# Hash-bucketed attention and a channel mix on one core: the planner's wanted times replaced by one written sequence

## The chip, the core and the metric

The kernel runs on one core of a Trainium2 chip. Five engines matter: PE (TensorE, matmuls), ACT (ScalarE), DVE (VectorE), POOL (GpSimd) and SP (SyncE, which here only issues DMAs). Each engine takes its own instructions in program order; an instruction whose input is not there holds everything behind it on that engine. The metric is the device time of one execution in microseconds (us). Before the change it is 253.47 us, the median of three runs (252.47 to 254.20).

## The reference, cut to what matters

```python
q_bits = (q @ proj > 0); k_bits = (k @ proj > 0)      # q, k, v: (4, 8, 768, 64); proj: (64, 6)
mask   = q_bucket[..., :, None] == k_bucket[..., None, :]   # buckets: the 6 bits as a number
attn   = softmax(where(mask, q @ k.T / 8, -1e9))
x      = (attn @ v), heads side by side: (4, 768, 512)
xk, xr = mu * x + (1 - mu) * x_prev                   # x_prev: the row before
k      = relu(xk @ w_k) ** 2                          # w_k: (512, 1024)
out    = sigmoid(xr @ w_r) * (k @ w_v)                # w_r: (512, 512), w_v: (1024, 512)
```

The 32 heads are worked on in 16 pairs; four pairs (0 to 3, 4 to 7 and so on) make one batch, and one batch can enter the channel mix when its four pairs are through.

## The kernel before, in words

**Work of one pair n.** SP loads q, k (lines 485, 491; names `ldq`n with side q or k) and v (line 496, `ldv`n) in fp32. DVE splits q and k into a high and a low fp16 part (`hi`, line 560; `lo`, line 563), SP transposes them by DMA (`tr`, line 567; one for q, one for k). PE computes the sign bits of the hash (`bits`, line 586), DVE turns them into fp16 values (`bx`, line 589), and four small DMAs put them as extra rows under q and k (`row`, line 599; a and b for the two heads of q, c and d for those of k). Then nine score steps of 1024 columns follow (`sc`, line 702), each with one exponential on ACT (`exp`, line 706). Six groups of matmuls apply v (`oo`, line 732), DVE divides (`rc`, `ob`), the result is transposed (`ot` on PE, line 758, or by a DMA, line 764), and DVE mixes it with the row before (`df`, `xk`, `xr`, lines 789 to 804). For v, POOL adds up the columns (`va`, `vsum`, lines 511 to 523) and PE makes the mean (`mean`, line 536). Pairs 0 and 1 have their q and k transposed by PE instead (lines 620 to 645), and pair 0 gets its bits in place (lines 662 to 670).

**Work of one batch.** 16 groups of four matmuls with w_k (`kp`, line 822), a relu on ACT and a square on DVE for each (lines 826, 829), 6 groups with w_r and a tanh (`r`, lines 841, 844), 12 groups with w_v (`v`, line 851), 6 products on DVE (line 858) and 6 stores (line 861).

**Weights.** w_k comes by four casting DMAs that POOL issues (`wg`, line 446); w_r and w_v come in fp32 by SP (`wl`, line 463) and POOL casts them (line 470).

**What sets the order.** The function writes all 1328 operations with `add(engine, duration, priority, function, reads, writes, ...)`. `Plan.schedule` (lines 159 to 284) then runs through them with a model of time: at each moment each engine takes the ready operation with the lowest wanted time, and the wanted time of operation i is entry i of the list `WANT` (lines 44 to 101). A DMA of more than 0.3 us is held back while the modelled queue has more than `BACKLOG` = 1.5 us of work. The operations are emitted in the order in which the model started them (lines 883 to 886), so the model fixes the order on each engine, and the bank of PSUM that each matmul group writes (`plan.slot`): three pairs of banks for score steps and `bits`, four banks for the rest, of which the channel mix holds at most three.

At most eight DMAs of SP and ACT are in flight, one for each of eight semaphores.

Of the kernel before, what the change touches and what calls it, by code (L numbers as in the profile page):

```python
# [17 lines left out]
LAG = {"PE": 0.30, "ACT": 0.25, "DVE": 0.20, "POOL": 0.20, "SP": 1.8, "GQ": 2.0}  # L18


BACKLOG = 1.5

# [17 lines left out]
def R(kind, n):  # L40
# [3 lines left out]
WANT = [  # L44
    2, 8, 6, 12, 18, 10, 26, 38, 44, 24, 5, 11, 30, 34, 35, 23, 36, 3, 33, 14, 32, 22, 0, 9,
    25, 1, 39, 42, 45, 48, 49, 46, 59, 31, 112, 84, 74, 63, 101, 324, 348, 401, 425, 387, 414, 455, 482, 379,
    403, 446, 470, 4, 41, 13, 37, 102, 21, 7, 117, 47, 50, 52, 51, 65, 66, 53, 19, 58, 40, 54, 17, 68,
    71, 76, 80, 62, 67, 73, 77, 56, 82, 89, 95, 104, 98, 69, 15, 78, 83, 90, 103, 64, 75, 175, 115, 123,
    135, 133, 61, 57, 72, 87, 28, 27, 70, 60, 96, 86, 100, 79, 29, 20, 55, 16, 107, 110, 134, 120, 127, 119,
    106, 131, 43, 91, 99, 105, 81, 88, 118, 109, 122, 132, 113, 130, 125, 129, 97, 141, 144, 148, 121, 157, 159, 154,  # L50
    161, 155, 166, 167, 170, 176, 179, 181, 188, 185, 108, 85, 221, 137, 147, 152, 156, 94, 92, 128, 93, 126, 114, 158,
    169, 194, 174, 187, 173, 172, 145, 150, 163, 164, 171, 178, 162, 153, 168, 142, 146, 143, 160, 139, 151, 138, 140, 190,
    198, 197, 207, 208, 177, 195, 183, 180, 204, 237, 220, 230, 233, 246, 241, 192, 182, 281, 191, 196, 206, 210, 124, 136,
    149, 111, 116, 165, 186, 193, 227, 202, 228, 211, 214, 184, 257, 262, 231, 238, 239, 244, 219, 217, 226, 218, 189, 200,
    205, 216, 201, 199, 267, 268, 271, 274, 275, 234, 236, 242, 252, 253, 279, 288, 297, 305, 300, 311, 203, 229, 298, 240,
    245, 250, 255, 222, 224, 248, 209, 212, 235, 273, 277, 302, 286, 299, 294, 247, 256, 243, 249, 276, 285, 260, 265, 263,
    269, 283, 295, 251, 270, 278, 290, 225, 215, 315, 292, 280, 291, 318, 293, 296, 307, 319, 323, 330, 334, 338, 341, 345,
    349, 350, 357, 362, 374, 383, 393, 392, 420, 424, 428, 434, 437, 380, 386, 398, 417, 427, 435, 433, 441, 448, 495, 504,
    516, 413, 423, 429, 431, 449, 454, 452, 461, 468, 450, 527, 533, 439, 444, 459, 500, 507, 522, 512, 519, 541, 520, 536,
    539, 485, 492, 525, 546, 550, 597, 497, 514, 558, 563, 566, 607, 542, 560, 562, 567, 572, 638, 578, 586, 594, 649, 616,  # L60
    939, 530, 581, 625, 635, 650, 925, 656, 664, 613, 642, 686, 913, 266, 213, 356, 301, 308, 312, 322, 332, 327, 336, 232,
    223, 259, 254, 258, 272, 284, 304, 329, 328, 343, 316, 346, 352, 333, 344, 351, 360, 325, 335, 339, 408, 317, 331, 310,
    289, 313, 321, 303, 309, 402, 407, 405, 418, 421, 363, 367, 369, 372, 375, 340, 467, 494, 506, 502, 543, 503, 517, 337,
    365, 426, 314, 320, 326, 342, 355, 353, 361, 282, 287, 347, 261, 264, 306, 376, 381, 396, 404, 391, 412, 410, 416, 395,
    406, 399, 411, 359, 368, 422, 430, 388, 397, 354, 373, 384, 390, 370, 378, 471, 475, 508, 490, 524, 457, 462, 469, 473,
    478, 371, 599, 620, 626, 637, 641, 629, 639, 477, 364, 532, 377, 382, 385, 438, 440, 443, 463, 358, 366, 415, 389, 409,
    432, 481, 487, 509, 528, 501, 513, 515, 523, 419, 436, 442, 451, 488, 496, 505, 510, 445, 456, 460, 464, 465, 472, 476,
    480, 529, 535, 499, 545, 547, 583, 585, 593, 602, 606, 466, 612, 628, 633, 647, 655, 644, 678, 484, 511, 553, 447, 453,
    458, 474, 483, 479, 486, 498, 491, 518, 394, 400, 489, 551, 559, 574, 569, 584, 565, 549, 554, 538, 540, 557, 576, 651,
    659, 631, 654, 627, 634, 573, 592, 589, 600, 587, 596, 675, 679, 684, 691, 694, 660, 665, 668, 673, 683, 493, 706, 735,  # L70
    739, 743, 749, 746, 753, 808, 817, 825, 819, 828, 834, 788, 801, 810, 779, 787, 809, 827, 839, 848, 849, 857, 865, 833,
    843, 847, 872, 878, 884, 786, 852, 860, 876, 882, 887, 851, 861, 866, 886, 905, 902, 867, 871, 880, 906, 909, 916, 894,
    897, 901, 864, 908, 911, 783, 797, 923, 935, 953, 1003, 769, 784, 919, 940, 945, 952, 962, 968, 955, 966, 973, 995, 988,
    989, 1035, 1039, 1044, 1049, 999, 1005, 974, 992, 1010, 1017, 1048, 1057, 930, 949, 1061, 1063, 537, 580, 652, 548, 552, 556, 577,
    579, 582, 588, 521, 526, 561, 531, 534, 544, 617, 622, 657, 636, 630, 646, 610, 614, 671, 677, 666, 669, 619, 624, 621,
    632, 604, 609, 648, 653, 601, 605, 640, 645, 693, 713, 715, 718, 721, 688, 701, 704, 708, 710, 590, 772, 793, 794, 796,
    803, 800, 806, 570, 591, 643, 568, 571, 575, 663, 670, 667, 676, 555, 564, 623, 603, 611, 661, 705, 712, 737, 729, 750,
    725, 698, 702, 690, 695, 720, 722, 717, 723, 711, 714, 733, 741, 728, 731, 742, 748, 680, 687, 738, 744, 747, 757, 762,
    758, 752, 767, 771, 773, 681, 781, 812, 814, 821, 831, 818, 836, 618, 755, 917, 672, 682, 685, 696, 699, 703, 707, 595,
    598, 674, 608, 615, 692, 724, 730, 740, 760, 766, 778, 813, 820, 782, 792, 770, 776, 822, 829, 775, 790, 763, 768, 754,  # L80
    764, 751, 756, 761, 777, 856, 842, 841, 858, 862, 798, 802, 815, 823, 826, 709, 895, 915, 920, 921, 927, 924, 1054, 732,
    853, 824, 689, 697, 700, 719, 726, 727, 734, 658, 662, 716, 774, 780, 791, 859, 868, 881, 890, 873, 877, 830, 835, 845,
    850, 869, 874, 883, 891, 879, 885, 795, 804, 855, 863, 837, 846, 805, 811, 899, 918, 934, 937, 938, 893, 896, 898, 910,
    912, 736, 959, 976, 979, 981, 985, 1059, 1066, 1076, 1080, 1085, 1047, 1051, 1071, 1072, 1078, 1082, 1062, 1070, 1075, 1124, 1130, 1134,
    1084, 1090, 1101, 1087, 1093, 1098, 1095, 1108, 1115, 1135, 1141, 1144, 1064, 1106, 1111, 1086, 1100, 1104, 1092, 1120, 1123, 1149, 1156, 1158,
    1131, 1137, 1140, 1119, 1125, 1129, 1112, 1127, 1132, 1154, 1162, 1147, 1187, 1194, 1196, 1146, 1152, 1181, 1185, 1186, 1190, 1193, 1200, 1199,
    1206, 1208, 1211, 1217, 1221, 1161, 1170, 1223, 1227, 1224, 1229, 1232, 1238, 1242, 1246, 1220, 1226, 1235, 1234, 1240, 1243, 765, 807, 816,
    936, 941, 944, 961, 967, 970, 977, 759, 745, 844, 889, 892, 903, 943, 948, 965, 969, 956, 991, 947, 951, 926, 933, 900,
    904, 907, 914, 971, 975, 980, 984, 1004, 1009, 922, 928, 997, 1001, 1007, 1008, 1015, 1019, 1026, 1020, 1023, 1027, 1032, 1036, 983,
    1040, 1053, 1056, 1065, 1069, 1073, 1077, 799, 888, 986, 946, 950, 954, 990, 993, 996, 1000, 785, 789, 832, 838, 840, 854, 958,  # L90
    963, 972, 998, 982, 978, 1011, 1018, 987, 994, 1025, 1028, 1030, 1037, 1034, 1046, 1055, 1068, 1081, 1088, 1089, 1103, 1060, 1067, 1058,
    1094, 1107, 1113, 1117, 1122, 1126, 1128, 1133, 1136, 1002, 1139, 1153, 1155, 1157, 1160, 1159, 1163, 957, 960, 964, 1014, 1024, 1021, 1029,
    870, 875, 929, 931, 932, 942, 1097, 1099, 1105, 1116, 1102, 1110, 1045, 1052, 1013, 1022, 1050, 1074, 1118, 1121, 1091, 1096, 1142, 1145,
    1079, 1083, 1109, 1114, 1143, 1148, 1138, 1150, 1151, 1165, 1164, 1166, 1171, 1174, 1177, 1178, 1031, 1182, 1192, 1195, 1201, 1203, 1198, 1230,
    1006, 1012, 1016, 1033, 1038, 1041, 1042, 1184, 1189, 1197, 1202, 1191, 1188, 1180, 1183, 1173, 1175, 1204, 1207, 1168, 1172, 1176, 1179, 1169,
    1167, 1205, 1209, 1212, 1214, 1216, 1210, 1213, 1215, 1218, 1219, 1043, 1222, 1225, 1228, 1231, 1236, 1239, 1233, 1237, 1250, 1244, 1256, 1245,
    1249, 1251, 1255, 1260, 1262, 1248, 1252, 1254, 1261, 1266, 1268, 1258, 1263, 1265, 1264, 1269, 1271, 1253, 1257, 1259, 1278, 1283, 1286, 1273,
# [5 lines left out]

class Op:
    pass


class Plan:

    def __init__(self, pairs, banks, most, moe_most):
        self.ops = []
        self.writer = {}
# [39 lines left out]
    def schedule(self):  # L159
# [31 lines left out]
        t = 0.0  # L191
# [726 lines left out]
```

## Time and profile before

| | |
|---|---|
| time, median of 3 runs | 253.47 us (252.47 to 254.20) |
| the profiled execution: its span, which is the only time recorded of it | 249.4 us |
| median of the runs less that span | 4.1 us |
| instructions | 6171 |
| PE busy, PE weight loads busy | 235.4 us, 140.4 us |
| DVE, ACT, POOL busy | 185.9, 183.2, 49.8 us |
| DMA moved | 43.5 MB, 174 GB/s on average |
| first exponential starts, last one of pair 3 ends | 12.73 us, 52.53 us |
| first `kp` group of batch 0 starts, last matmul ends | 60.76 us, 245.50 us |

How to read it: times count from the start of the span. Operations are named as above (`sc2_0` is step 0 of pair 2); their times come from the trace, by the order of the instructions on each engine. "Lands" means that the semaphore of a DMA has reached its full count.

### The profile page before, as it was taken

The numbers are of one execution on the slowest core, as the hardware profiler recorded it, in microseconds if no ns is written. First come the engines' busy times: TensorE is split into PE (matmuls) and PEld (weight loads), VectorE is DVE, ScalarE is ACT, GpSimd is POOL, SyncE is SP. The second block draws the span as 40 slices with busy tenths as digits, with TensorE's granted clock in tenths as the row PEclk, the third lists the DMA queues.
The fourth block names the chain that finished last, engine by engine and source line by source line (L and its number), as shares of the span: only waits on it lengthen the run. The fifth ranks groups of instructions, "written<-read, shape, count | busy, mean of one in ns | idle before, by whom it ended". The sixth has DMA issues, their size and how long they took to land.

```text
span 249.4 us, 6171 instructions
## 1 busy us (share of the span) xinstructions
PE 235.4 (94%) x2453; PEld 140.4 (56%) x2453; DVE 185.9 (75%) x415; ACT 183.2 (73%) x242; POOL 49.8 (20%) x89
## 2 busy tenths in 40 slices
PE   7897988897999999999999999999999999999993
PEld 3344654474667555558666666447666666555441
DVE  4997599899986987899989976786856626854321
ACT  3589859869999845899799988169997677247210
POOL 7209142245364123004100000522000000000000
PEclk9799999999999999999999999999999999999999
DMA  7994999998999999989968999945210103220123
GB/s 204 265 314 88 170 277 224 236 231 221 310 216 323 246 266 232 270 235 216 137 206 208 223 215 205 267 74 196 74 42 9 34 9 108 87 84 3 42 84 128
DMA packets 73341, 43.50 MB, mean 174 GB/s; under 512 B 55544, under 2 KB 68192, under 8 KB 73312
## 3 DMA queue, kind: packets, MB, share of 16 engines
q1 hardware_dynamic: 72656, 42.05, 68.8%
q0 software_dynamic: 576, 1.05, 2.3%
q8 instruction: 19, 0.31, 0.5%
q14 instruction: 10, 0.08, 0.1%
q10 hardware_dynamic: 80, 0.00, 0.0%
HBM read 24.12 MB, written 6.29 MB: 122 GB/s over the span
## 4 chain that ended last, share of the span: by engine, by line
PE 77%; DMA 7%; ACT 6%; DVE 3%; SPq 3%; issue 2%; DVEq 0%; ACTq 0%
PE ps_all L702 18%; PE ps_all L851 17%; PE ps_all L822 17%; PE ps_all L732 13%; PE ps_all L841 8%; ACT pt L706 6%; DMA nat<-in_k_dram 5%; PE ps_all L586 3%; DMA a<-bx 3%; SPq L599 2%; DVE bx L589 1%; SPq L567 1%; SPq L491 1%; DVE a L643 1%; DVE nh L625 0%
## 5 line engine op out<-in xcount | busy, mean ns | idle before, releaser
L706 ACT ACTIVATE pt<-ps_all 128x1024 bf16<-128x1024 f32 x144 | 140.6, 1042 | 24.0 <-PE ps_all L702 22.4
L702 PE MATMUL ps_all<-a 128*128 128x512 f16 (+1 forms) x384 | 81.3, 325 | 6.2 <-ACT pt L706 3.5
L702 PEld LDWEIGHTS <-a 128*128 128x128 f16 x384 | 33.6, 97 | 33.1 <-issue 10.4
L732 PEld LDWEIGHTS <-pt 128*128 128x128 bf16 x1152 | 43.6, 97 | 8.5 <-ACT pt L706 0.8
L822 PE MATMUL ps_all<-xk,wk 128*128 128x384 bf16 x256 | 47.4, 326 | 0.0
L851 PE MATMUL ps_all<-wv,k 128*128 128x512 bf16 x192 | 46.8, 379 | 0.0
L732 PE MATMUL ps_all<-va,pt 128*128 128x65 bf16 x1152 | 45.6, 193 | 0.3 <-ACT pt L706 0.2
L826 ACT ACTIVATE kr<-ps_all 128x384 bf16<-128x384 f32 x64 | 30.8, 509 | 7.8 <-PE ps_all L822 4.7
L822 PEld LDWEIGHTS <-wk 128*128 128x128 bf16 x256 | 24.3, 98 | 16.2 <-issue 1.0
L829 DVE TENSOR_TENSOR k<-kr 128x384 bf16<-128x384 bf16 x64 | 22.4, 359 | 14.1 <-ACT kr L826 13.7
L517 POOL TENSOR_TENSOR vt<-vn 128x384 f32<-128x384 f32 x12 | 12.7, 1060 | 90.5 <-DMA vn<-in_v_dram 90.2
L844 ACT ACTIVATE rs<-ps_all 128x512 f32<-128x512 f32 x24 | 14.4, 604 | 22.2 <-PE ps_all L841 15.4
L851 PEld LDWEIGHTS <-k 128*128 128x128 bf16 x192 | 18.4, 98 | 20.1 <-issue 0.3
L858 DVE SCALAR_TENSOR_TENSOR os<-rs,ps_all 128x512 f32<-128x512 f32 x24 | 16.5, 686 | 17.4 <-PE ps_all L851 11.9
L563 DVE SCALAR_TENSOR_TENSOR nh<-nat,nh 128x768 f16<-128x768 f32 x28 | 28.7, 1033 | 0.3
L841 PE MATMUL ps_all<-wr,xr 128*128 128x512 bf16 x96 | 24.5, 379 | 0.0
L560 DVE TENSOR_SCALAR nh<-nat 128x768 f16<-128x768 f32 x28 | 16.3, 583 | 3.9 <-DMA a<-nh 1.5
L748 DVE TENSOR_TENSOR ob<-ps_all,rc 128x384 bf16<-128x384 f32 x32 | 17.7, 554 | 0.7
L589 DVE TENSOR_SCALAR bx<-ps_all 128x768 uint16<-128x768 uint16 x15 | 14.3, 954 | 1.3 <-PE ps_all L586 0.8
L841 PEld LDWEIGHTS <-xr 128*128 128x128 bf16 x96 | 8.8, 98 | 8.8 <-issue 0.3
L586 PE MATMUL ps_all<-a,p 128*32 128x256 f16 (+1 forms) x240 | 13.0, 328 | 0.5 <-DMA a<-nh 0.3
L542 DVE SCALAR_TENSOR_TENSOR va<-ps_all,vn 128x384 bf16<-128x384 f32 x24 | 12.2, 547 | 0.9 <-PE ps_all L537 0.9
(69 smaller groups left out, 157.5 us busy)
## 6 DMA issues: line engine op xcount, KB each, us to landing
vn<-in_v_dram SPq DMA_DIRECT2D x16, 384.0 KB
out_dram<-os SPq DMA_DIRECT2D x24, 256.0 KB
nat<-in_k_dram SPq DMA_DIRECT2D x15, 384.0 KB
nat<-in_q_dram SPq DMA_DIRECT2D x15, 384.0 KB
wk<-in_moe_w_k_dram POOLq DMA_DIRECT2D x4, 256.0 KB, 8.3
wst<-in_moe_w_r_dram SPq DMA_DIRECT2D x2, 512.0 KB
wst<-in_moe_w_v_dram SPq DMA_DIRECT2D x2, 512.0 KB
a<-bx SPq DMA_DIRECT2D x60, 9.0 KB
```

The costliest lines, as they stand in the source:

```text
L563: nc.vector.scalar_tensor_tensor(out=nh[:, :, D:P], in0=nat.rearrange("p j (c d) -> p (j c) d", d=D), scalar=QS, in1=nh[:, :, 0:D], op0=AL ...
L586: nc.tensor.matmul(ps[32 * i : 32 * i + 32, lo:hi], w_, a_t[sa][:, i, lo:hi], start=st, stop=not st)
L589: nc.vector.tensor_scalar(out=bx_t[sx].bitcast(U16), in0=ps_t[plan.slot[nm]][:, 0:S].bitcast(U16).rearrange("p (c e) -> p c e", e=2)[:, :, 1],
L702: nc.tensor.matmul(ps[:, lo - s * STEP : hi - s * STEP], side_a["k"][sa][:, j, jc * P : (jc + 1) * P], side_a["q"][sa][:, j, q0 : q0 + hi ...
L706: nc.scalar.activation(out=pt_t[sp][:, s * STEP : (s + 1) * STEP], in_=ps_t[plan.slot[nm]], func=AF.Exp, bias=EBIAS, scale=ESC)
L732: nc.tensor.matmul(oo[:, ic * 65 : ic * 65 + 65], pt_t[sp][:, o : o + P], va_t[sa][:, j, jc, 0 : D + 1], start=(not uc and ic == 0 and jc ...
L748: nc.vector.tensor_tensor(out=ob_t[so][:, :, j * D : (j + 1) * D], in0=oo[:, :, 0:D], in1=rc_t[sr][:, 1, :].unsqueeze(2).to_broadcast([P, ...
L822: nc.tensor.matmul(ps[:, 0:HALF], wk_sb[:, d, fc * P : (fc + 1) * P], xk_t[mx[d]][:, h * HALF : (h + 1) * HALF], start=(d == 0), stop=(d = ...
L826: nc.scalar.activation(out=kr_t[sk], in_=sm(nm)[:, 0:HALF], func=AF.Relu, scale=0.5 ** 0.5)
L829: nc.vector.tensor_tensor(out=k2_t[s2][:, h * HALF : (h + 1) * HALF], in0=kr_t[sk], in1=kr_t[sk], op=ALU.mult)
L841: nc.tensor.matmul(sm(nr), xr_t[mx[d]][:, c * P : (c + 1) * P], wr_sb[:, d, :], start=(d == 0), stop=(d == NDC - 1))
L851: nc.tensor.matmul(sm(nv), k2_t[(b * NFC + fc) % NK2][:, c * P : (c + 1) * P], wv_sb[:, fc, :], start=(fc == 0), stop=(fc == NFC - 1))
```

## The change

The list of wanted times becomes a list `ORDER` of all 1328 operations, and the planner goes through it from front to back. The operations themselves (their instructions, shapes and buffers) are the same; the order on each engine and the choice of banks are new. Figures of the model (durations, lags, times of landing, the port that DVE and POOL share, half-tiles as separate keys for xk and xr) change too; since the order is now written down, they only decide which free bank a matmul group takes.

```diff
-LAG = {"PE": 0.30, "ACT": 0.25, "DVE": 0.20, "POOL": 0.20, "SP": 1.8, "GQ": 2.0}
-BACKLOG = 1.5
+LAG = {"PE": 0.21, "ACT": 0.21, "DVE": 0.15, "POOL": 0.18, "SP": 1.8, "GQ": 2.0}
-WANT = [
-    2, 8, 6, 12, 18, 10, 26, 38, 44, 24, 5, 11, 30, 34, 35, 23, 36, 3, 33, 14, 32, 22, 0, 9,
...
+ORDER = [
+    37, 51, 0, 25, 17, 2, 3, 4, 5, 14, 6, 7, 11, 8, 53, 24, 59, 13, 1, 21, 22, 36, 60, 10,
...
+    def sequence(self):
+        if ORDER:
+            return [self.ops[i] for i in ORDER]
...
     def schedule(self):
...
+        order = self.sequence()
+        for o in order:
+            e = "POOL" if o.eng == "GQ" else o.eng
...
+            if o.take is not None:
...
+                choices = [(max(t, *(bank_free[b] for b in bs)), k, i, bs) for k, (i, bs) in enumerate(choices) if not any(used[b] for b in bs)]
+                t, _, self.slot[name], bs = min(choices)
...
-            add("GQ", 0.7, ..., w=[("wk", c0)], at=0.75, svc=1.66, off=2.2, name=f"wg{i}")
+            add("GQ", 0.7, ..., w=[("wk", c0)], at=0.75, svc=1.7, off=4.1, name=f"wg{i}")
```

What moves, by places in the queues (counted from 0):

| queue | before | after |
|---|---|---|
| POOL | memsets, identity, hash tables, then `wg2 wg1 wg0 wg3` at 21 to 24 | `wg2` at 0, `wg1` at 9, `wg0` at 14, `wg3` at 20, small work between |
| SP, start | `ldq0q0 ldq1k ldq0k0 ldq1q mur ldq0k1 ldq0q1 muk ldq2q ldq2k ldq3k ldv0 ldq3q ldv1`, `row1` d, b, c, `tr2`, `row1` a | the four loads of pair 0, `muk ldq1k ldq1q ldq2q ldv2 ldv0 ldq2k ldq3q ldq4q tr2 ldq3k ldv3`, `row1` d, b, `tr2 ldv1`, `row1` c, a |
| ACT | the dummy exponential (`table`, line 410) at 1 | at 200 |
| DVE, start | high and low parts of pair 1's k at 3, 4, 5, 8 | at 10, 12, 16, 17, behind those of pair 0 |
| DVE | `xk0` at 46, `xr2` at 79, `xk3` at 90 | at 73, 113, 87 |
| PE | `sc3_8` at 64, `bits9` at 184, `bits15` at 339, first `kp` at 103, `v1_5b` at 290 | at 87, 174, 317, 106, 367 |

## The prediction

> **What bounds the kernel now.** First the windows view, cut at places that the next views gave. Its columns are start:end, length, then busy time and count of PE, PEld, DVE, ACT and POOL, then the granted clock, the DMA share and GB/s.
>
> ```profile
> 0.00:12.00 12.00, 9.23 (x50) 3.93 (x51) 8.00 (x20) 4.75 (x9) 5.74 (x31) 0.86 0.89 235
> 12.00:34.00 22.00, 19.04 (x262) 11.98 (x260) 17.53 (x29) 18.23 (x20) 7.48 (x9) 1.00 0.91 206
> 34.00:62.00 28.00, 24.00 (x300) 14.85 (x296) 26.15 (x46) 24.14 (x27) 12.20 (x15) 1.00 0.93 231
> 62.00:125.00 63.00, 62.66 (x747) 38.97 (x747) 55.07 (x131) 52.44 (x69) 17.07 (x23) 1.00 1.05 244
> 125.00:187.00 62.00, 62.00 (x650) 37.84 (x647) 48.60 (x119) 51.85 (x72) 7.29 (x12) 1.00 0.73 172
> ```
>
> From 62 us on PE is never idle, at full clock; all of its idle time lies before. Busy PE is not PE at its peak, so I also took the time from one matmul's start to the next, when nothing holds it: 144 score steps of 0.431 us, 96 `oo` groups of 0.378, 64 `kp` of 0.650, 24 `r` and 48 `v` of 0.863, 15 `bits` of 0.766 and 14.7 for the rest make 228.3 us. The last matmul starts at 244.47, so 244.47 − 228.3 = 16 to 17 us are lead and stalls. At the first `kp` (60.76, with 45.5 us of such work done) the loss is already 15.3. So a gain has to come from the first 62 us, and has to be kept afterwards. In those 62 us the chain of work that ended last says what was late:
>
> ```profile
> 1.66 4.15 DMA nat<-in_k_dram
> ...
> 10.21 7.12 DMA nat<-in_k_dram
> ...
> 18.02 0.97 DVE bx L589
> 19.01 0.84 SPq L599
> ...
> 21.32 1.54 SPq L567
> 22.91 2.57 DMA a<-bx
> ...
> 33.30 4.61 DMA a<-bx
> ...
> 54.67 0.78 ACT pt L706
> ```
>
> Loads at the start, the bits of pair 1 (`bx`) at 18.02, SP issuing its rows one after the other, the rows in flight; the same again for pair 2 at 33.30, then exponentials. The waits of ACT (12:62) and of PE (whole span) agree: ACT, at 0.905 us from start to start, stands still between pairs.
>
> ```profile
> ACT pt L706 <- PE ps_all L702: 7.0, 7, 2.6
> ```
> ```profile
> PE ps_all L702 <- ACT pt L706: 3.5, 9, 1.3
> PE ps_all L702 <- DMA a<-bx: 1.8, 2, 1.3
> ```
>
> Last the DMA queues in 12.5:13.5, and the window 19:22.5:
>
> ```profile
> q0 software_dynamic: 117, 0.22, 115.1%
> q1 hardware_dynamic: 1, 0.00, 0.1%
> ```
> ```profile
> 19.00:22.50 3.50, 2.17 (x11) 0.99 (x11) 3.47 (x4) 3.50 (x5) 3.26 (x4) 1.00 0.08 25
> ```
>
> When POOL's casting queue (q0) runs, SP's queue (q1) gets nothing, with two loads waiting. And at 19 to 22.5 the engines of the DMA stand still (0.08), since SP's next entry is a row that waits for `bx1`.
>
> **The change part by part.** No instruction, DMA or wait on data is added or removed; only places move.
>
> *Casting loads first.* `wg2` goes from 5.15 to about 0.75 (POOL place 0), `wg1`, `wg0`, `wg3` to about 2.6, 4.6 and 6.3, by the POOL work between them. Before, the first packets came at 8.0 and the full rate at 9.0, 3.9 after the issue, and one casting load takes about 1.3 us of DMA time. Pair 0's four loads still come before that: the first landed at 3.2 and a 384-KB load takes 1.0 to 1.1, with half-sized ones about 0.6, so they land at 3.2, 3.8, 4.4, 5.0 (before, its last came at 8.0). `ldq1q`, next but two on SP, would land at 7.4 (3.2 + 3×0.6 + 0.2 for `muk` + 1.15 + 1.05). With two whole casts and part of a third in front I take L = 10.6. Bounds: 7.4 (none in front) and about 14 (all four, and what they hold up).
>
> What waits for it: on DVE `hi1q0` at place 13, with 14 operations of the start behind it, among them `bx1`; PE's `t1k10` (place 18) stands ahead of `sc0_3`. From L to the end of `bx1` DVE has 2 `hi` of 0.31, 4 `lo` of 0.47, 5 copies of 0.475, and 0.49, 0.88, 0.96, 0.875 after: 8.1 us. So `bx1` ends at 18.7, against 18.98 before: L up to 10.9 costs nothing, and the bounds make it 15.5 to 22.1. DVE cannot use an early 15.5 in full, since `ldq1k` is before it and pair 0's exponentials run on; I bound the gain there by 1 us, the loss by 3. The first exponential comes at about 10.5 rather than 12.73, but the ninth only at about 18.6.
>
> *SP's order.* `ldq3q`, `ldq4q`, `tr2`, `ldq3k` and `ldv3` now stand ahead of the rows of pair 1. Four loads of 1.05 us and a transpose of 1.4 fill the gap of 3.2 us (3.5 × 0.92), and put the rows behind them: I take `row1` d and b at 24.2 (before 21.0 and 21.7, 2.5 later) and the last, a, at 27.2 (before 25.5). That is the price. The return: the same loads are not in front of pair 2 and 3. Pair 1's exponentials run 24.8 to 33.0 (9 × 0.905), pair 2's rows land at 32 to 33.8 (before 33.7 to 37.9), its exponentials run 33 to 41.2 (before 34.74 to 47.03), pair 3's rows come at 38.7 to 41.8, its exponentials end at about 50 (before 52.53), and pair 4's run 50.5 to 59 (before 54.67 to 63.41). Pair 4 is 4 us earlier, and PE's loss, at 47 us of work, about 10 rather than 15.2. Each of these starts is the later of "rows landed" and "ACT free"; SP's queue is served in order throughout.
>
> *What is given back.* PE can only go on at this lead if the inputs of pairs 5 to 7 come. Place 153 on PE is `sc7_8`, needing `row7b`, with 69.3 us of PE work before it. Before, `row7b` landed at 90.3. I count DMA work in units of one 384-KB load (1 for a load, 1.4 for a transpose, 0.25 for a row set): 47.3 units from 33.5 to 90.3 took 56.8 us, 1.2 us each. In the new order 62.4 units go up to `row7b`, of which 10.6 are done at 20 us; the other 51.8 at the same pace bring it at 82.1. So PE's loss there is 82.1 − 69.3 = 12.8 us. With the pace of a queue never idle (1.08 each) it is about 76, and ACT's pace is then the bound, at a loss of about 11; with the landing times of before moved by no more than the filled gap, 85, which is 15.7, all of the loss of before. I take 12.8, the mean pace, since the change fills one gap and not all. Gain against 15.7 at the same 69.3 of work: 2.9 us.
>
> *After 70 us.* `bits9` and `bits15` come 9 and 15 us of PE work earlier, and `kp` and `v` groups correspondingly later. Where `tr10` is needed (107 to 110 us), its DMA lands at 105 to 109 by the same count: margin about 0. Summing DVE's and ACT's durations up to each operation that PE needs, DVE is 0.3 to 2.4 us of work ahead after the change (1.5 to 16 before), ACT between 0.3 behind and 1 ahead (0.2 to 2.6 ahead before). PE's only wait there before was this (62:250):
>
> ```profile
> PE ps_all L702 <- ACT pt L706: 0.3, 2, 0.2
> ```
>
> I take 0 for new stalls, since the sums still close; with DVE 5 to 8% slower than its means over some 100 us of its work they would cost 5 to 8 us, which I keep for the upper end. Below nothing isn't possible: 0.3 us is all that PE loses there.
>
> *Edits at nothing.* The dummy exponential at ACT place 200 leaves the table load (1.28 us) to the first real ACTIVATE. The load's row:
>
> ```profile
> 1.32 1.28 ACT L410 ACT_TABLE_LOAD   x1 [1.32 <-PEq L902]
> ```
>
> It ran at 1.32, ahead of any input, and the next ACTIVATE began 1.30 after it. Even behind the first K load it ends at 3.9 + 1.28, its conversion at 5.7, before DVE is through with its first parts at 6.1; if that cover is gone, 1.3 us. `xk0`, `xr2` move back on DVE: their reader `kp0` had 4.9 us of cover, and has 2.0. `mur` on SP goes behind 20 others and `wl` is still cast before its first `r` or `v`. The stores `st0` go later; the three `os` buffers cover that as long as DVE's products are 3 groups of 0.86 apart. The last 20 operations of PE are the same, so is the tail of 4.1 us to the median.
>
> **Two rules of the Trainium skill.** "ScalarE: Activation LUTs", What ACT_TABLE_LOAD costs, gives 1283 ns for the load, which the row has, and a drain of some 1380 ns when it stands right ahead of an ACTIVATE, which the row (1.30 to the next start) does not show. By that rule the late load would cost an estimated 1.0 us more at the first conversion, and the sum would be 251.6. "Perfetto Trace Analysis", Identifying the Most-Contended Engine, would have PE judged by its weight loads, 56% here, and not by 94%: by that rule there is room for far more than 3 us. The start-to-start sum says it is at most the 17 us of lead and stalls.
>
> **The rivals.** (a) *Slower.* DVE's thin lead in the second half runs out; each late `xk`, `va` or square holds PE, which is in order. For it: DVE is 55.07 of 63 us busy in 62:125, and now has its work drawn earlier. Against: from 62 us to the end DVE stood 13.7 us waiting for ACT's relus, so it has room. Price 5 to 8 us: 255.6 to 258.6. It decides once DVE's sums are over 5% short. (b) *Same.* `ldq1q` waits for all casts (L = 14): `bx1` at about 22, three us later, which eats the 2.9; or the rows behind the prefetch land at the 85 curve. 252 to 254.5. For it: the 115.1% against 0.1%. (c) *More.* Dense DMA: loss 11 and less at `sc7_8`; PE at 247 to 248.5. For it: the share 1.05 in 62:125. (d) *It does nothing*: order was already near what the data allow, 253.5; the 17 us of loss speak against it.
>
> **How the numbers follow.** Span 249.4 − 2.9 = 246.5; with the same 4.1 around it 250.6. The forecast's own range is 249.2 to 251.9: 1.3 us to either side, what 0.025 us per unit makes over the 51.8 units. Chances: forecast 0.40, (a) 0.24, (b) 0.18, (c) 0.16, (d) 0.02. A measurement of this kernel tells about 1% (2.5 us): faster is under 250.9, slower over 256.0. Of the forecast's 0.40 some 0.26 lie under 250.9, with (c)'s 0.16 that is 0.42. Slower is (a) and a hundredth of (b), 0.25. The rest, 0.33, is between. The range reaches from (c)'s fast end, 246.8, into (a), to 257.0: of (a) about 0.13 lies above, of (c) 0.03 below.
>
> **What would show it.** First exponential at 10 to 11; `wg2` on the queue at 4.6; DVE's `hi1q0` waiting for a load until 10 to 11 and `bx1` ending near 18.7; a DMA share above 0.6 in 19:22.5; `row1` d landing near 24; pair 4's first exponential near 50.5; `sc7_8` near 82; PE's waits after 62 under 1 us. A first exponential later than 12.7 or `bx1` after 21 makes (b); PE waits for DVE after 80 make (a).

## The result, and the profile after

The changed kernel is slower: 262.59 us (261.35 to 264.27, four runs) against 253.83 us (252.47 to 255.42); ratio 1.0339, 95% interval 1.0288 to 1.0391, or 8.6 us. The forecast was 250.6.

The profiled execution after has a span of 260.6 us and a time of 262.37, so 1.8 us lie around a span, not the 4.1 that the prediction set against the median. The profiled execution of before, span 249.4, would so be one of 251.2 us, below all four of its timed runs; the same queues, profiled again in the first experiment, gave a span of 254.0. Of the 11.2 us between the two pages some 2.6 (11.2 less 8.6) are therefore chance. Sizes below are taken from the timed ratios; the traces show where they arise.

The windows view after, with the cuts and columns of before:

```profile
0.00:12.00 12.00, 7.50 (x31) 3.32 (x32) 4.04 (x10) 3.91 (x6) 5.41 (x27) 0.87 0.83 186
12.00:34.00 22.00, 17.13 (x188) 10.41 (x189) 18.60 (x32) 15.88 (x19) 7.68 (x11) 0.91 1.03 247
34.00:62.00 28.00, 24.83 (x369) 16.43 (x368) 23.41 (x42) 24.69 (x27) 7.34 (x14) 1.00 0.92 223
62.00:125.00 63.00, 59.21 (x701) 37.36 (x705) 52.49 (x113) 53.50 (x69) 19.02 (x23) 1.00 0.95 217
125.00:187.00 62.00, 58.07 (x675) 36.18 (x678) 47.47 (x112) 52.85 (x67) 8.28 (x12) 0.97 0.77 166
```

DVE does half as much in the first 12 us (4.04 against 8.00 us) and ACT falls back in the next 22. And PE, which missed 0.3 us between 62 and 187 before, now misses 3.8 and 3.9 us in these two windows. PE's waits from 62 us to the end name what for:

```profile
PE ps_all L651 <- DMA a<-bx: 5.6, 3, 2.7
PE ps_all L535 <- DMA a<-nh: 1.0, 1, 1.0
PE ps_all L771 <- DVE mc L498: 0.4, 1, 0.4
```

PE waits for rows of bits (`a<-bx`) and for a transpose (`a<-nh`): transfers, and hardly DVE. The chain of work that ended last, over the whole span, has them one by one:

```profile
3.62 10.60 DMA nat<-in_q_dram
...
21.06 6.43 DMA nat<-in_k_dram
...
56.35 3.34 DMA a<-bx
...
75.36 4.73 DMA a<-nh
...
84.28 7.16 DMA a<-bx
...
125.71 1.85 DMA a<-bx
...
137.94 4.66 DMA a<-bx
```

The first is `ldq1q`, in flight for 10.6 us; then come a load of pair 3, a row of pair 4, a transpose of pair 7, `row7b` (7.16 us from issue to landing; 2.7 before) and rows of pairs 10 and 11.

To put all runs on one scale I use PE's loss: the time at which a matmul group starts, less all PE work queued ahead of it by the start-to-start times of the prediction. (20 of the 2453 matmul records are missing in the trace after, at `r` and `v` groups; there the weight load's start stands in.) The table counts about 1.8 us less of the small matmuls in the first 15 us than the prediction's sum, so all its losses stand 1.8 us above the prediction's: the 15.3 us at the first `kp` of before are 17.1 here. Differences between rows are not affected. In the trace of the profiled execution the loss is, in us, at so many us of PE work:

| | 15 | 45 | 65 | 85 | 115 | 225 | ratio of times to before, interval |
|---|---|---|---|---|---|---|---|
| before | 8.7 | 17.4 | 17.6 | 17.8 | 18.7 | 19.2 | 1 |
| its queues again (`ctl`) | 10.6 | 19.7 | 20.0 | 20.2 | 22.5 | 23.8 | 1.0026 [0.9977, 1.0074] |
| after | 12.5 | 20.4 | 21.9 | 24.3 | 29.5 | 30.6 | 1.0339 [1.0288, 1.0391] |
| after, half loads | 13.0 | 19.8 | 20.7 | 20.9 | 21.2 | 21.9 | 1.0009 [0.9974, 1.0043] |
| before, half loads | 8.2 | 17.1 | 18.0 | 18.1 | 18.9 | 19.4 | 0.9884 [0.9840, 0.9928] |
| before, casts first | 15.3 | 24.4 | 25.8 | 25.9 | 28.5 | 29.1 | 1.0256 [1.0180, 1.0333] |

At 45 us of work, after has lost 1 to 3 us more than the two profiles of before's queues. From there on it loses 10 us, where those lose 2 and 4.

### The profile page after: what moved, and what is told of

Read it like the earlier page. It is cut to its first block, busy times and chain, and to the rows that moved or that the text cites. A ratio compares the mean times of both kernels' runs of the same rounds, so it can differ in the third digit from the quotient of the medians.

```text
span 260.6 us, 6173 instructions
## 1 busy us (share of the span) xinstructions
PE 236.1 (91%) x2433; PEld 141.5 (54%) x2453; DVE 188.4 (72%) x415; ACT 183.7 (71%) x242; POOL 49.6 (19%) x89
## 3 DMA queue, kind: packets, MB, share of 16 engines
q0 software_dynamic: 576, 1.05, 2.4%
## 4 chain that ended last, share of the span: by engine, by line
PE 63%; DMA 17%; DVE 11%; SPq 5%; issue 3%; ACT 1%; DVEq 0%; ACTq 0%
PE ps_all L800 15%; PE ps_all L771 14%; PE ps_all L651 14%; PE ps_all L681 8%; PE ps_all L790 7%; DMA a<-bx 7%; DMA nat<-in_k_dram 4%; DMA nat<-in_q_dram 4%; PE ps_all L535 3%; DVE nh L512 2%; SPq L548 2%; DMA a<-nh 2%; DVE nh L509 2%; DVE ob L697 1%; DVE xk L744 1%
## 5 line engine op out<-in xcount | busy, mean ns | idle before, releaser
L771 PE MATMUL ps_all<-xk,wk 128*128 128x384 bf16 x256 | 49.4, 329 | 0.5 <-DVE mc L498 0.4
L681 PEld LDWEIGHTS <-pt 128*128 128x128 bf16 x1152 | 42.0, 97 | 7.2 <-issue 0.8
L800 PE MATMUL ps_all<-wv,k 128*128 128x512 bf16 x178 | 45.2, 379 | 0.7
L681 PE MATMUL ps_all<-va,pt 128*128 128x65 bf16 x1152 | 43.5, 193 | 0.0
L771 PEld LDWEIGHTS <-wk 128*128 128x128 bf16 x256 | 24.4, 98 | 18.6 <-issue 2.3
L778 DVE TENSOR_TENSOR k<-kr 128x384 bf16<-128x384 bf16 x64 | 23.8, 391 | 13.4 <-ACT kr L775 13.4
L466 POOL TENSOR_TENSOR vt<-vn 128x384 f32<-128x384 f32 x12 | 13.3, 1107 | 105.8 <-DMA vn<-in_v_dram 105.6
L512 DVE SCALAR_TENSOR_TENSOR nh<-nat,nh 128x768 f16<-128x768 f32 x28 | 27.7, 993 | 0.5
L790 PE MATMUL ps_all<-wr,xr 128*128 128x512 bf16 x90 | 23.5, 379 | 0.3
L697 DVE TENSOR_TENSOR ob<-ps_all,rc 128x384 bf16<-128x384 f32 x32 | 17.8, 557 | 1.0
L509 DVE TENSOR_SCALAR nh<-nat 128x768 f16<-128x768 f32 x28 | 15.6, 562 | 2.4 <-DMA nat<-in_k_dram 2.4
```

The source lines that it names most:

```text
L509: nc.vector.tensor_scalar(out=nh[:, :, 0:D], in0=nat.rearrange("p j (c d) -> p (j c) d", d=D), scalar1=QS, scalar2=None, op0=ALU.mult)
L512: nc.vector.scalar_tensor_tensor(out=nh[:, :, D:P], in0=nat.rearrange("p j (c d) -> p (j c) d", d=D), scalar=QS, in1=nh[:, :, 0:D], op0=AL ...
L681: nc.tensor.matmul(oo[:, ic * 65 : ic * 65 + 65], pt_t[sp][:, o : o + P], va_t[sa][:, j, jc, 0 : D + 1], start=(not uc and ic == 0 and jc ...
L697: nc.vector.tensor_tensor(out=ob_t[so][:, :, j * D : (j + 1) * D], in0=oo[:, :, 0:D], in1=rc_t[sr][:, 1, :].unsqueeze(2).to_broadcast([P, ...
L771: nc.tensor.matmul(ps[:, 0:HALF], wk_sb[:, d, fc * P : (fc + 1) * P], xk_t[mx[d]][:, h * HALF : (h + 1) * HALF], start=(d == 0), stop=(d = ...
L778: nc.vector.tensor_tensor(out=k2_t[s2][:, h * HALF : (h + 1) * HALF], in0=kr_t[sk], in1=kr_t[sk], op=ALU.mult)
```

## The experiments

The theory after the comparison has two causes: a late start (casting loads and prefetched loads in front of pair 1) and transfers that come late for pairs 7, 10 and 11. Its rivals are another choice of banks; one cause, the start, with the rest passed on; SP's time to issue; and DVE, for which PE's waits above leave 0.4 us after 62 us.

### Which part of the change

`ctl`: the planner of after with the sequence of before.

```diff
-ORDER = [37, 51, 0, 25, ...]     # after
+ORDER = [...]                    # the sequence in which before emits
```

> The sequence of before, written out as ORDER and run through the planner of after: every engine has the queue of before, only the choice of PSUM banks is made with the new figures. If banks don't matter: 253.8 within 1.0 us. If the new choice of banks carries part of the loss: 256 or more.

Measured: 1.0026 [0.9977, 1.0074]. With the old sequence, the new choice of banks makes no difference clear of noise.

`b62_a` and `a62_b`: spliced sequences.

```diff
+ORDER = BEFORE[:360] + [i for i in AFTER if i not in BEFORE[:360]]     # b62_a
+ORDER = AFTER[:334] + [i for i in BEFORE if i not in AFTER[:334]]      # a62_b
```

> The first 360 operations of before's sequence (its first 62 us), then the rest in the order of the change. Theory two causes: the loss of PE after 62 us (8.1 of the 11.4 us between the two traces) belongs to the later order and stays; time 257 to 261. Rival one cause: the late order only passes on a late start; time 253 to 255.

> The first 334 operations of the changed sequence (its first 62 us), then the rest in the order of before. Theory two causes: only the 3.3 us lost up to the first kp group stay; time 256 to 258.5. Rival one cause (the late start makes all that follows late): 261 to 263.

Measured: 1.0305 [1.0190, 1.0419] and 1.0430 [1.0331, 1.0530]. With the start of before the loss at 45 us of work is 17.9, as before, and it still grows to 30.1, with the same wait at `sc11_5` (2.2 us). So the later order loses by itself, and the rival of one cause falls. The other splice missed what both theories expected: after the first 62 us of the changed order, the transfers of the old order come at the wrong time (`row5c` holds PE for 3.8 us), and it tells only that the halves can't be exchanged at will. Since it cuts at such a seam too, `b62_a` alone (4.6 us of its loss arise at `kp0_2_1` and `r0_0`, just behind the seam) doesn't size the later part; the half loads below do.

### The start

`a_wg_back`: after, with the casts where before has them. `a_wgback_row1`: also pair 1's rows ahead of the prefetch. `b_wg_first` and `b_wg_late`: before, with the casts alone moved.

```diff
 POOL (a_wg_back):  -wg2 .. wg1 .. wg0 .. wg3 between the small work    +small work, wg2 wg1 wg0 wg3
 SP (a_wgback_row1, too):
-ldq3q ldq4q tr2 ldq3k ldv3 row1d row1b tr2 ldv1 row1c row1a
+ldq3q row1d row1b row1c row1a ldq4q tr2 ldq3k ldv3 tr2 ldv1
 POOL (b_wg_first): -wg2 wg1 wg0 wg3 at 21 to 24      +at 0, 9, 14, 20
 POOL (b_wg_late):  -wg2 wg1 wg0 wg3 at 21 to 24      +behind vsum0c, vsum1c, vsum2c, vsum3c
```

> The changed kernel with one edit: the four casting loads wg stand behind POOL's small work of the start (first issue at about 5 us instead of 1.24). Theory casts: they hold up the second heads of pair 0 (landed 7.5 to 7.7) and both loads of pair 1 (12.0 and 14.2); without them in front bx1 ends 2 to 4 us before 23.7 and the time falls by 2.5 to 4.5 us, to 258 to 260. Rival prefetch: the loads that SP has ahead of the rows of pair 1 cost it; then 262.6 within 1.

> The changed kernel with two edits at the start: the casting loads back behind POOL's small work, and the four rows of pair 1 on SP ahead of ldq4q, tr2, ldq3k, ldv3, tr2, ldv1. Theory overlap: the casts and the prefetch each alone hold pair 1 at 28 us (with the casts moved back, rows issued at 20.5 still landed at 26.0); with both gone its rows land at 22.5 to 24, its exponentials begin at 24.7 or earlier, and the time falls by 2.5 to 4.5 us against the changed kernel (ratio 1.016 to 1.024 to before). Rival late part: the loss after 70 us is set by the inputs of pairs 7 and 11 and takes up whatever the start gives; ratio 1.028 to 1.036.

> The kernel before with only the four casting loads moved to the changed kernel's POOL places 0, 9, 14 and 20. Theory casts: they take the DMA before pair 0's and pair 1's loads are in; bx1 ends 2 to 4 us after 18.98 and the time grows by 2 to 4 us (ratio 1.008 to 1.016). Rival: their data move in gaps; ratio within 0.995 to 1.005.

> The kernel before with only the four casting loads moved behind POOL's vsum0c, vsum1c, vsum2c and vsum3c (21.9 to 45 us instead of 5.1 to 6.9; first reader kp0 at 60.8). Theory casts: pair 2's and 3's loads land 2 to 4 us earlier, bx1 ends 1 to 3 us before 18.98 and the time falls by 1 to 4 us (ratio 0.984 to 0.996). Rival: the 5 us of casting come later between rows and transposes and cost the same there; ratio 0.997 or more.

Measured: 1.0265 [1.0143, 1.0387], 1.0330 [1.0233, 1.0426], 1.0256 [1.0180, 1.0333], 1.0336 [1.0244, 1.0428]. Against the 1.0339 of the changed kernel, the first gain is not clear of noise, and the second, for which the theory had 1.016 to 1.024, is none.

The casts alone (`b_wg_first`) cost 6.5 us, more than the 2 to 4 expected. Its chain (0:30) shows how:

```profile
3.16 10.40 DMA nat<-in_k_dram
...
24.60 0.97 DVE bx L538
...
26.48 1.85 DMA a<-bx
```

Pair 0's second K load was in flight for 10.4 us and `bx1` ended at 25.6 instead of 19.0; the 6.6 us lost by 15 us of work stay (7.0 at 45). The change pays less for them (3.8 us by 15 us of work): it also brings pair 0's loads forward, and the last of them landed at 7.7 instead of 14.0.

With the casts back in the changed kernel, `bx1` ends at 20.5 and pair 0's exponentials begin at 11.2; but row d, issued at 20.5, lands at 26.0, behind `ldq4q`, `tr2` and the loads after them, and pair 1's exponentials begin at 28.2, as with the casts in front (28.0). So the prefetch alone keeps pair 1 until 28 us; the casts alone do so in before's order (29.1 in `b_wg_first`), and the two delays overlap. With both undone they begin at 24.3, and then PE waits 3.9 us for the transpose of pair 2 that the rows have displaced (PE's waits, 0:62, of `a_wgback_row1`):

```profile
PE ps_all L535 <- DMA a<-nh: 3.9, 1, 3.9
PE ps_all L651 <- DMA a<-bx: 2.1, 3, 1.1
```

`b_wg_late` went the other way than I expected: 8.5 us slower. Its windows show why nothing is won:

```profile
16.00:20.00 4.00, 2.11 (x22) 1.10 (x21) 3.91 (x6) 2.81 (x3) 3.72 (x6) 1.00 0.26 39
19.00:22.50 3.50, 1.46 (x7) 0.58 (x6) 3.47 (x5) 2.63 (x3) 3.26 (x5) 1.00 0.48 80
```

All loads had landed at 15.9 (20.3 before), and the DMA stood at 0.26, but `bx1` ended at 20.06: it waits for the chain of transposes and bits through DVE, ACT and PE, not for loads, and SP's rows wait for it. The old place of the casts filled this hole; later they stand among rows and transposes (`row1a` took 4.4 us to land, 2.6 before). PE's waits for rows up to 62 us (0:62) are 6.5 us, where before had 1.8 in its whole span:

```profile
PE ps_all L651 <- DMA a<-bx: 6.5, 4, 2.4
```

Another wait of 2.3 us for a row comes at 112 us (`sc8_0`), 56 us after the last cast has landed; its cause I have not followed.

### The later part

`a_rows`: rows and a transpose ahead of loads at the two waits.

```diff
-ldv7 ldq9q wl8 wl9 ldq9k ldv8 row7d row7a row7b
+ldv7 ldq9q wl8 row7d row7a row7b wl9 ldq9k ldv8
-tr11 otd7 row10d row10b tr11 .. ldq13k ldv11 ldv12 ldq14k ldq13q row11d row11a row11b .. row11c
+tr11 tr11 otd7 row10d row10b .. ldq13k row11d row11a row11b row11c ldv11 ldv12 ldq14k ldq13q ..
```

> The changed kernel with SP's queue changed at two places after 75 us: rows d, a, b of pair 7 ahead of wl9, ldq9k, ldv8; the second transpose of pair 11 ahead of otd7, and its rows ahead of ldv11, ldv12, ldq14k, ldq13q. Theory rows behind loads: PE's waits at sc7_8 (2.2 us) and sc11_5 (2.9 us) go, and the time falls by 3.5 to 5 us: ratio 1.014 to 1.020. Rival pace: SP issues without a pause anyway (31.7 of 38 us busy between 62 and 100), so a wait that is taken away at one place comes back at another; ratio 1.027 or more.

Measured: 1.0478 [1.0415, 1.0541], slower than after. PE's waits from 62 us on:

```profile
PE ps_all L651 <- DMA a<-bx: 3.3, 2, 2.0
PE ps_all L535 <- DMA a<-nh: 2.9, 1, 2.9
PE ps_all L771 <- DVE bx L538: 1.1, 1, 1.1
```

The waits at `sc7_8` and `sc11_5` are gone, and others stand in their place: `row7c` (1.5 us), `row10b` (2.1), `bits12` behind its second transpose (2.9). My theory that the rows merely stood in the wrong place falls. It looks like a shortage, in which the order only chooses who pays.

What is short? `a_rowpool` and `b_rowpool` give SP less to issue. `a_half` and `b_half` give the DMA engines fewer bytes at the same issues: from pair 5 on, the loads of q, k and v leave out the second head, which then computes on what stood in the buffer.

```diff
-nc.sync.dma_start(out=a_t[sa][D : D + NB, i, :], ...)
+(nc.gpsimd if n >= 2 and i % 2 else nc.sync).dma_start(out=a_t[sa][D : D + NB, i, :], ...)
```

```diff
+h = 1 if n >= 5 else 2
-nc.sync.dma_start(out=side_nat[side][s], in_=SRC[side][b, 2 * t : 2 * t + 2]...)
+nc.sync.dma_start(out=side_nat[side][s][:, 0:h], in_=SRC[side][b, 2 * t : 2 * t + h]...)   # v likewise
```

> The changed kernel with rows b and d of pairs 2 to 15 issued by POOL instead of SP: 28 issues of 0.70 us, some 20 us, less in SP's queue, the same bytes. Theory SP: SP's issuing (31.7 of 38 us between 62 and 100) sets when pairs 7, 10 and 11 come; the time falls by 3 to 6 us (ratio to before 1.010 to 1.022). Rival transfer: the 16 DMA engines set it (share 0.95 in 62:125); within 1.5 us of the changed kernel, ratio 1.027 to 1.040.

> The sequence of before with rows b and d of pairs 2 to 15 issued by POOL. Theory SP: 1 to 4 us faster than before (0.984 to 0.996). Rival transfer: 0.996 to 1.006; a row behind POOL's sums of v could also make it slower.

> The changed kernel with the loads of q, k and v of pairs 5 to 15 cut to their first head (half the bytes; the second head computes on what stood in the buffer): SP's issues unchanged, 16.5 loads' worth of DMA time less. Theory transfer: PE's waits for rows and transposes after 62 us go; ratio 0.985 to 1.005. Theory SP: they stay; ratio 1.025 to 1.035.

> The sequence of before with the same loads cut to one head: the yardstick for the run on the changed kernel. PE waited only 0.36 us after 62 us here, so little can be won: 0.985 to 1.0. If the changed order itself (what PE asks for when) is the cause and the transfers only serve it, the changed kernel with half loads comes to the same time as this one.

Measured: `a_rowpool` 1.0572 [1.0508, 1.0637], `b_rowpool` 1.0115 [1.0062, 1.0168], `a_half` 1.0009 [0.9974, 1.0043], `b_half` 0.9884 [0.9840, 0.9928].

The rows on POOL don't decide, and both kernels are slower for them: POOL's queue holds the rows behind sums that wait for v (its timeline, 80:150, of `a_rowpool`), which I had named for `b_rowpool` and not priced.

```profile
89.39 1.19 POOL L466 TENSOR_TENSOR vt<-vn 128x384 f32<-128x384 f32 x1 [2.42 <-DMA vn<-in_v_dram]
90.53 1.11 POOL L548 DMA_DIRECT2D a<-bx  x2
...
139.52 1.09 POOL L466 TENSOR_TENSOR vt<-vn 128x384 f32<-128x384 f32 x1 [12.76 <-DMA vn<-in_v_dram]
```

The half loads do. With SP's issues unchanged in number, PE waits for no row or transpose after 62 us (`a_half`, two views: PE's waits from 62 us on, and the window 62:100):

```profile
PE ps_all L487 <- DVE ob L699: 0.3, 1, 0.3
PE ps_all L773 <- DVE mc L500: 0.3, 1, 0.3
```
```profile
62.00:100.00 38.00, 37.16 (x440) 23.55 (x444) 33.77 (x72) 36.39 (x50) 15.61 (x18) 1.00 0.87 196
```

The same bytes taken from before win 1.2%; from after, 3.3%. So 2.1% (5.4 us) of the 3.4% is waiting for transfers that only the new order has. The other 1.25% (1.0009 against 0.9884, 3.2 us) is the start, which the half loads hardly touch (in `a_half` the first of them is issued at 33.3 us): in the table the two kernels with half loads differ by 2.7 us at 45 us of work and by 2.5 at the end. One thing these runs don't tell apart: with fewer bytes, the issue of a transpose also holds SP for less (a median of 1.50 us instead of 2.35 in 62:125). They show that bytes are short, and not how much of it reaches PE through SP.

### What was still open

```diff
-h = 1 if n >= 5 else 2
+h = 1 if 5 <= n < 10 else 2      # a_half_5to9
+h = 1 if n >= 10 else 2          # a_half_10on
```

`a_half_wgback` and `a_half_wgback_row1` are the half loads with the orders of `a_wg_back` and `a_wgback_row1`.

> The changed kernel, loads of q, k and v cut to one head for pairs 5 to 9 only. Two shortages: PE's wait at sc7_8 goes, that at sc11_5 stays; 3 to 5 us off, ratio 1.014 to 1.022. One cause passed on: the waits at pairs 10 and 11 go too; ratio 1.000 to 1.008. Cutting the middle merely moves the shortage back: 1.025 or more.

> The changed kernel, loads cut to one head for pairs 10 to 15 only. Two shortages: sc7_8 stays at 2 to 3 us, the wait at sc11_5 goes; 3.5 to 6 us off, ratio 1.010 to 1.020. One cause: the delay at pair 7 makes the later waits and 8 us stay or only 1 us goes; ratio 1.028 or more.

> The changed order with half loads from pair 5 on and the casting loads back behind POOL's small work. Theory overlap (casts and prefetch both hold pair 1 until 28 us): little comes of the one alone; ratio 0.996 to 1.003. Rival casts alone: all of the difference to the order of before with half loads; 0.985 to 0.993.

> As the run before it, with the rows of pair 1 ahead of ldq4q, tr2, ldq3k, ldv3, tr2, ldv1 on SP. Theory overlap: 0.984 to 0.993, the time of the order of before with half loads or better. Rival: the second transpose of pair 2, now late, holds bits2 on PE (4.9 us in the full-load run); ratio 1.000 to 1.008.

Measured: 1.0114 [1.0007, 1.0222], 1.0171 [1.0120, 1.0222], 0.9946 [0.9908, 0.9984], 1.0024 [0.9978, 1.0070].

Halving pairs 5 to 9 takes the wait at `sc7_8` away and leaves 1.7 us at `sc11_5`; halving pairs 10 to 15 leaves `sc7_8` (1.6 us) and takes `sc11_5` away. The gains, 2.25% and 1.7%, add up to a little more than the 3.3% of both, well within the intervals. So they are two shortages, not one delay passed on. At the start, the casts make half of the 1.25% (1.0009 to 0.9946, between what the theory and its rival had; the intervals overlap by 0.1%). The trace doesn't show where: the profiled execution of `a_half_wgback` was its slowest, and at 50 us of work it had lost no less than that of `a_half` (20.6 and 20.1). The rows ahead of the prefetch win nothing on top, as the rival had it: PE waits 3.9 us inside `bits2` for the second transpose instead. The other half of the start's loss I couldn't put on one edit.

## Why the prediction was wrong, step by step

The sum had one term, a gain of 2.9 us up to pair 7, and 0 for everything behind it. The runs have 3.2 us lost at the start and 5.4 us lost to late transfers from pair 5 on, both against before.

**Casting loads first: the step that failed at the start.** I let `ldq1q` land at 10.6 with "two whole casts and part of a third in front"; it landed at 14.23, behind all four (`wg3` at 13.74): my upper bound, 14. I had 1.3 us for one cast; they landed at 7.3, 9.9, 11.9 and 13.7, 1.8 to 2.6 apart. I also had pair 0's second heads at 4.4 and 5.0, ahead of any casting; they landed at 7.48 and 7.74. The DMA queues of after in 4.5:7.5:

```profile
q0 software_dynamic: 139, 0.25, 50.6%
q1 hardware_dynamic: 703, 0.37, 46.1%
```

Casting already takes half the engines' time there. In 8:12.5 it is 70.7%, beside 39.0% for SP's queue. So a cast slows SP's loads; that SP's queue "gets nothing" I had read from a single us of before, and over 9:16 of before the shares were 79.2% and 30.8%. DVE stood waiting (its timeline, 0:20):

```profile
7.50 0.36 DVE L569 TENSOR_SCALAR nh<-nat 128x384 f16<-128x384 f32 x1 [3.37 <-DMA nat<-in_q_dram]
...
12.03 0.36 DVE L569 TENSOR_SCALAR nh<-nat 128x384 f16<-128x384 f32 x1 [1.65 <-DMA nat<-in_k_dram]
...
14.25 0.36 DVE L569 TENSOR_SCALAR nh<-nat 128x384 f16<-128x384 f32 x1 [0.88 <-DMA nat<-in_q_dram]
```

The first exponential came at 14.6 (10.5), `bx1` ended at 23.70 (18.7, bound 22.1). The break-even I gave, L = 10.9, was 3 us below what happened. That is the mechanism of rival (b), but its price was half of what was needed: its 3 us only eat the gain of 2.9, while the start ended 3.2 us above before.

**SP's order.** The gap was filled as I said; the DMA share in 19:22.5 is 0.74 (0.08):

```profile
19.00:22.50 3.50, 3.50 (x40) 1.97 (x38) 2.78 (x5) 2.43 (x3) 2.84 (x5) 0.97 0.74 172
```

But the rows of pair 1 landed at 25.9 to 31.8 (24.2 to 27.2), its exponentials ran 28.0 to 37.9 (24.8 to 33.0), pair 4's began at 56.3 (50.5). PE's loss at 47 us of work was 18.6 and not 10 (on the prediction's scale). The return on the prefetch, 4 to 5 us, never came: filling the idle DMA in front of the rows delayed them, and `b_wg_late` shows that the idle DMA was not what pair 1 waited for.

**What is given back: the step that failed at pair 7.** `row7b` landed at 91.4, not 82.1: the 51.8 units took 1.38 us each from 20 us on, not 1.2. PE's loss at `sc7_8` was 22.3 us, not 12.8. I took before's mean pace as a property of the queue. It is the pace of one order. In after the engines stood idle in places where before kept them full (75:80 and 100:110, after and then before):

```profile
75.00:80.00 5.00, 4.12 (x53) 2.68 (x49) 4.54 (x13) 4.88 (x8) 1.37 (x3) 1.00 0.66 129
100.00:110.00 10.00, 9.95 (x87) 5.34 (x87) 8.16 (x18) 7.93 (x11) 1.82 (x3) 1.00 0.64 196
```
```profile
75.00:80.00 5.00, 5.00 (x79) 3.76 (x78) 2.82 (x11) 5.00 (x9) 1.86 (x4) 1.00 1.11 337
100.00:110.00 10.00, 10.00 (x76) 5.11 (x74) 9.31 (x20) 8.66 (x10) 0.00 (x0) 1.00 0.97 249
```

SP, in order, waited for `bx6` (1.9 us), `bx8` (1.6), `bx9` and the low parts of pairs 7 and 10 (0.8 each) with loads behind them. By 100 us, 27 loads of 384 KB had landed (29 before); by 125 us, 18 transposes of q and k (21 before) and 36 rows (38 before). Meanwhile PE came to pair 7 with 69.2 us of its work done, where before had 74.4. That SP's waits cause the dips is read from the trace; no run removed them alone.

**After 70 us: the step that failed behind it, priced at 0.** It was about 6 us (24.3 to 30.6 at 85 and beyond), most of it at `sc11_5` (2.9) and `sc10_5` (1.0). I had weighed DVE's and ACT's margins and found the transfers' margin "about 0" at `tr10`, and then priced a margin of 0 at nothing. `row11b` landed 13 us later than before (142.6, 129.2).

Such a wait also cost more than its own length. The groups right behind `sc11_5` lost another 1.5 us, with no wait listed there, while the granted clock was 0.50 (the window 143:145):

```profile
143.00:145.00 2.00, 2.00 (x9) 0.97 (x7) 0.00 (x0) 0.03 (x1) 0.00 (x0) 0.50 0.79 215
```

A lower clock shows at the start, too: 0.91 in 12:34, where before has 1.00. In `a_half`, which lacks the wait at `sc11_5`, the clock in 125:150 is 1.00 (0.93 after). No run changed the clock without the waits, so what it adds by itself is not shown.

**Rivals.** (a) had the sign, 255.6 to 258.6, and the wrong engine: after 62 us DVE was never what PE waited for, beyond 0.4 us. (b) had the mechanism of the start, at half its price, and nothing for the later part. (c) supposed a denser DMA, which this order didn't bring: its share in 62:125 is 0.95 (1.05 before).

**Edits at nothing.** They held. The table load ran at 1.32 as before, though the dummy stands at place 200:

```profile
1.32 1.28 ACT L571 ACT_TABLE_LOAD   x1 [1.32 <-PEq L851]
3.66 0.52 ACT L571 ACTIVATE nh<-nat 128x384 f16<-128x384 f32 x1 [1.06 <-DMA nat<-in_k_dram]
```

It isn't tied to its ACTIVATE in time, and the idle 1.06 us between the two end with the load of K. So the 1.0 us that the prediction worked out from the rule on the table load isn't there. Nor would the other rule, to go by the weight loads' 56%, have found the loss; the start-to-start sum did. Only the cover of `xk` was thinner than the 2.0 us I gave it: `kp0_0_1` came 0.6 us late, behind `xk3`.

**The frame.** The 4.1 us around the span are 1.8. This didn't move the sum: the median less 2.9 is the same 250.6.

## What to carry to other kernels

Here a transfer's landing depended on everything issued before it, so the mean pace of one order couldn't date the transfers of another: follow each critical transfer through what it waits for and what stands ahead of it. A margin of zero in an in-order queue is a cost, not a zero: price it with the wait that comes if the transfer is a few us late. And an idle slice of a resource is only worth filling if somebody on the path waits for that resource; find that out by taking the load away, as the half loads and the late casts did here.

## What the runs showed that I had not expected

- The casting queue and SP's queue shared the engines' time at 50.6% to 46.1% in 4.5:7.5 of after and at 70.7% to 39.0% in 8:12.5, with 326 and 384 packets; in before's 12.5:13.5 casting had all of it, 115.1% to 0.1%.
- Of ten kernels that differed from before in order or issuing queue alone, none was faster; moving four casting loads earlier cost 2.6%, moving them later 3.4%. No version that loads all its data beats before.
- After PE had waited 2.7 us for a row, the granted clock fell: 0.71 in 140:145 of after, 1.00 in the same window of before.
